# Keys and queries of batches 3 to 7 turned by the DMA crossbar instead of TensorE, with two output banks

## The chip, the cores and the metric

One core of one Trainium2 chip. The metric is the device time of one execution in microseconds (us), the median of several runs; most runs of one kernel lie within 0.3% of each other. "PE" is TensorE, "ACT" ScalarE, "DVE" VectorE, "POOL" GpSimd, "SP" the sync engine, whose queue ("SPq") issues most transfers. "L502" is line 502 of the kernel that the profile belongs to; the line numbers of two kernels differ.

## The reference

Local attention with a few global positions, then a feed-forward layer with softplus. Batch 8, 8 heads, sequence 576, head size 64, window 32, 8 global positions:

```python
scores = scale * np.matmul(q, k.transpose(0, 1, 3, 2))
mask = np.abs(pos[:, None] - pos[None, :]) <= window
mask = mask | is_global[:, None] | is_global[None, :]
scores = np.where(mask, scores, -1000000000.0)
attn = np.exp(scores - max); attn = attn / (sum(attn) + 1e-09)     # shortened
x = np.matmul(attn, v).transpose(0, 2, 1, 3).reshape(4608, 512)
h = x @ w_in                                                        # 512 -> 2048
out = softplus(h) @ w_out                                           # 2048 -> 512
```

## The kernel before

TensorE does two things in turns. The feed-forward layer runs over nine tiles of 512 tokens, each with 32 groups of four 128x512 matmuls, half of them hidden products ("hp") and half output products ("o") of the tile before. Between the groups, half step by half step, lies the attention of later batches, one pair of heads at a time: transposes of keys and queries, scores, sums of the exponentials ("av<-ex,ones") and values. A plan says in which half step each part is issued:

```python
STARTS = [33, 39, 45, 51, 57, 63, 70, 76] + [83 + 8 * i for i in range(4 * (B - 4) + 1)]
...
h, pair = STARTS[4 * b - 8 + p], STARTS[4 * b - 7 + p] - STARTS[4 * b - 8 + p]
to_transposes, to_scores, to_sums = h, h + pair // 2 + (pair == 7), h + pair
to_inverse, to_x = to_sums + 1, to_sums + 2
...
step(to_transposes, transposes, "k", b, p)
step(to_transposes + (b > 1), transposes, "q", b, p)
for grp in range(2):
    step(to_scores, scores, b, p, grp)
...
step(to_sums, inv_ln, b, p)       # ACT: logarithm of the row sums
step(to_inverse, inv_exp, p)      # ACT: exp(-log), the inverse
step(to_x, scale_x, b, p)         # DVE: values times inverse, into xT
```

So a pair takes 6 half steps in batch 2, 6 or 7 in batch 3, and 8 from batch 4 on. A half step is one group of four products. Keys and queries of a pair are turned by six matmuls each, into one PSUM bank, from where VectorE copies them into `KT` and `QT`:

```python
for r in range(RUN):
    for o, of in parts:
        nc.tensor.transpose(out=tb[o, r * NQ:(r + 1) * NQ], in_=of(r), identity=ident_bf[:NQ, :NQ])
...
copy(dst[:, p, 0:4, 0:KW].rearrange("p t (q r) -> p t q r", r=RUN), ...)   # VectorE, PSUM to SBUF
cg(dst[:, p, :, KW:P], g.unsqueeze(1).to_broadcast([P, NTL, NG]))         # GpSimd, global columns
```

An output tile collects in one PSUM bank through four half steps, and is then copied by VectorE and stored:

```python
ops[n] = psum["pool"].tile([P, d_model], FP32, tag="h" if last else "o", bufs=2 if last else 1, name="o")
products_out(n, i, op[:], range(4 * part, 4 * part + 4))
if part == 3:
    store(n, i, op[:])
```

The softmax here doesn't subtract the row's maximum and nothing guards it: scores larger than these inputs give would overflow.

Of the kernel before, what the change touches and what calls it, by code (L numbers as in the profile page):

```python
# [19 lines left out]
P = 128  # L20
WIN = 32
KW = 120
# [18 lines left out]
def kernel(  # L41
# [37 lines left out]
    KT = const.tile([P, NP, NTL, P], BF16)  # L79
    QT = const.tile([P, NP, NTL, P], BF16)  # L80
    V1 = [const.tile([P, NTL, HD], BF16, name=f"V1_{i}") for i in range(2)]
    runs = const.tile([NQ, H, RUN * D], FP32, name="k_f")
    v_f = const.tile([P, NTL, HD], FP32)
    GB = B - 3
    glob_2 = {n: const.tile([P, NP, NG], BF16, name=f"{n}_g2") for n in "kq"}
# [23 lines left out]
    def load_v(b, heads=slice(0, H)):  # L109
        for t in range(NTL):  # L110
            nc.sync.dma_start(out=v_f[:ST[t], t].rearrange("p (h d) -> p h d", d=D)[:, heads],
                              in_=v[b, heads, KW * t:KW * t + ST[t], :].rearrange("h s d -> s h d"))

    def load_v_rows(b):
        nc.sync.dma_start(out=v_f[KW:P], in_=v_rows[:, (b - 1) * HD:b * HD].unsqueeze(1).to_broadcast([NG, NTL, HD]))
# [171 lines left out]
    def transposes(n, b, p, copy=nc.vector.tensor_copy, unread=0):  # L287

        parts = [(slice(0, P), lambda r: kqb[n, b][:, r, p * P:(p + 1) * P])]
        if n == "q" and b < 2:  # L290
            parts = [(slice(64 * e, 64 * e + 64), lambda r, e=e: raw[b][:, 2 * p + e, r * D:(r + 1) * D]) for e in range(2)]
        if b == 1 and p:
            if n == "k":
                both[p] = region("tp")
            ps = both[p][:, 0:512] if n == "k" else both.pop(p)[:, 512:1024]
        else:
            ps = bank()[:]
        tb = ps.bitcast(BF16)
        for _ in range(unread):
            nc.tensor.matmul(out=ps, lhsT=junk[:, 0:P], rhs=junk[:], start=True, stop=True)  # L300
# [3 lines that stand above are left out]
        if b < 2:  # L304
            g = ps[:, 384:384 + NG]
            for r in range(RUN):
                for o, of in parts:
                    nc.tensor.matmul(out=g[o], lhsT=of(r), rhs=onehot[:NQ, r, :],
                                     start=(r == 0), stop=(r == RUN - 1), skip_group_check=True)
        else:  # L310
            copy = nc.vector.tensor_copy
            g = glob_2[n][:, p] if b == 2 else glob_T[n][:, p].rearrange("p (g b) -> p b g", b=GB)[:, b - B + GB]
        spread = lambda: spread_columns(n, b, p, tb, g, copy)
        if b == 1 and p:
            both.setdefault((p, "copies"), []).append(spread)
            if n == "q":
                for f in both.pop((p, "copies")):
                    f()
        else:
            spread()  # L320
# [22 lines left out]
    def products(b, p, grp):  # L343
        sc = SC[p, grp] = region("sc")[:].rearrange("p (e c) -> p e c", e=2)
        biased = (b, p) in BIASED
        if biased:
            for e in range(2):
                nc.tensor.matmul(out=sc[:, e, 0:GW[grp]], lhsT=ident_bf[:], rhs=biases[grp], start=True, stop=False,  # L348
                                 skip_group_check=True)
        for i, t in enumerate(GRP[grp]):  # L350
            w = WHI[t] - WLO[t]
            for e in range(2):
                r = slice(64 * e, 64 * e + 64)
                nc.tensor.matmul(out=sc[:, e, GOFF[t]:GOFF[t] + w], lhsT=KT[r, p, t, :],  # L354
                                 rhs=QT[r, p].rearrange("p t c -> p (t c)")[:, WLO[t]:WHI[t]],
                                 start=not biased, stop=(not biased or i == len(GRP[grp]) - 1), skip_group_check=biased)

    def exponentials(b, p, grp):
# [151 lines left out]
    def mm2(n, s):  # L510
        i, part = s // 4, s % 4
        if part == 0:

            last = n == n_tiles - 1
            ops[n] = psum["pool"].tile([P, d_model], FP32, tag="h" if last else "o", bufs=2 if last else 1, name="o")
        op = ops[n]
        if n == n_tiles - 1 and i == NT // P - 1:
            if part % 2 == 0:
                cols = slice(0, 256) if part == 0 else slice(256, 512)
                if part:  # L520
                    op = psum["pool"].tile([P, d_model], FP32, tag="h", bufs=2, name="o")
                products_out(n, i, op[:, cols], range(KF), cols)
                store(n, i, op[:, cols], cols)
            return
# [3 lines that stand above are left out]
# [31 lines left out]
    for i, n in enumerate("kq"):  # L559
        at(14 + i, 0, columns_of_2, n)  # L560
        at(27, i, global_columns, n)
        for g in range(NG):
            at(18 + g, 0, gather_rows, n, g)
    LOADS, CASTS = {3: (18, 20, 19)}, {3: (23, 26)}
    for b in range(1, B):
        g0 = 16 * (b - 1)
        if b > 2:
            loads = LOADS.get(b, (g0 - 22, g0 - 20, g0 - 17))
            at(loads[0], 1, load_runs, "k", b, every)
            at(loads[1], 1, load_runs, "q", b, every)  # L570
            at(loads[2], 1, load_v, b)
            at(loads[2], 1, load_v_rows, b)
            casts = CASTS.get(b, (g0 - 12, g0 - 9))
            for p in range(NP):
                for i, n in enumerate("kq"):
                    at(casts[0] + (4 * i + p) // 3, 0, cast_runs, n, b, pair_heads(p), nc.gpsimd.tensor_copy)
            for t in range(NTL):
                at(casts[1] + t // 3, 0, cast_v, b, t, nc.gpsimd)
        steps = {}

        def step(h, f, *a):
# [2 lines left out]
        for p in range(NP):  # L584
            if b == 1:

                to_transposes, to_scores, to_sums = (2 if p == 1 else 4 * p + 2), 4 * p + 4, 4 * p + 6
                to_inverse = to_x = to_sums
            else:
                h, pair = STARTS[4 * b - 8 + p], STARTS[4 * b - 7 + p] - STARTS[4 * b - 8 + p]  # L590
                to_transposes, to_scores, to_sums = h, h + pair // 2 + (pair == 7), h + pair
                to_inverse, to_x = to_sums + 1, to_sums + 2
            if (b, p) != (1, 0):
                step(to_transposes, transposes, "k", b, p)
                step(to_transposes + (b > 1), transposes, "q", b, p)
                for grp in range(2):
                    step(to_scores, scores, b, p, grp)
                for grp in range(2):
                    if (b, p) not in BIASED:
                        step(to_scores, mask, p, grp)  # L600
            step(to_sums, sums, b, p)
            step(to_sums, values, b, p)
            step(to_sums, inv_ln, b, p)
            step(to_inverse, glob_sums, b, p, 0)
            step(to_inverse, inv_exp, p)
            step(to_x, scale_x, b, p)
# [143 lines left out]
```

## Time and profile before

| | us | share of the span |
|---|---|---|
| time, median of 3 | 361.45 | |
| span of the profiled run | 358.5 | |
| TensorE busy | 340.8 | 95% |
| ScalarE busy | 271.6 | 76% |
| VectorE busy | 169.2 | 47% |
| GpSimd busy | 130.9 | 37% |

The busy line, the chain, the cost of the transposes and the pair periods stand in the prediction below. Two more views are needed. First the page's line for the transfers and its row of DMA shares (forty slices of the span, in tenths): after the first quarter the DMA engines are about half free.

```profile
DMA  7999999999546155806590658100000010010012
DMA packets 63252, 37.87 MB, mean 106 GB/s; under 512 B 41688, under 2 KB 58496, under 8 KB 63216
```

Then TensorE's waits between 60 and 130 us (what it waited for: us in all, times, longest):

```profile
PE sc L354 <- DVE xT L436: 1.6, 4, 0.5
PE o L502 <- DVE ot L507: 0.9, 1, 0.9
PE tp L303 <- DVE KT L327: 0.6, 2, 0.3
```

### The profile page before, as it was taken

How to read it: one execution, taken by the hardware profiler on the slowest of the kernel's cores; microseconds unless marked ns; L12 is line 12 of the kernel's file. 1: busy time of each engine (PE TensorE's matmuls, PEld its weight loads, DVE VectorE, ACT ScalarE, POOL GpSimd, SP SyncE). 2: the span in 40 equal slices, each digit the busy share in tenths (PEclk: the TensorE clock that was granted, in tenths of full speed). 3: DMA queues.
4: the chain of work that ended last, by engine and by line, in shares of the span. 5: the costliest groups of instructions: out<-in, count | busy, mean ns of one | idle time of the engine just before them, and what ended most of it. 6: DMA issues, size and time to landing. Idle time of an engine off the chain costs nothing.

```text
span 358.5 us, 7702 instructions
## 1 busy us (share of the span) xinstructions
PE 340.8 (95%) x2957; PEld 174.5 (49%) x2997; DVE 169.2 (47%) x477; ACT 271.6 (76%) x425; POOL 130.9 (37%) x301
## 2 busy tenths in 40 slices
PE   7898998999899999999999999999999999999996
PEld 3465554544355545554555455545554444444444
DVE  7864532565566565655566556555553200010021
ACT  3676998788789888888888888888888677776610
POOL 7953947896177016431744075304000100000000
PEclk9999999999999999999999999999999999999999
DMA  7999999999546155806590658100000010010012
GB/s 173 234 219 221 214 195 232 85 204 196 96 89 115 35 145 93 166 31 155 97 172 29 163 96 161 42 29 33 29 31 31 30 59 29 31 56 32 31 59 88
DMA packets 63252, 37.87 MB, mean 106 GB/s; under 512 B 41688, under 2 KB 58496, under 8 KB 63216
## 3 DMA queue, kind: packets, MB, share of 16 engines
q1 hardware_dynamic: 44912, 27.63, 32.4%
q0 software_dynamic: 18160, 9.75, 20.9%
q8 instruction: 23, 0.38, 0.5%
q14 instruction: 13, 0.11, 0.1%
q10 hardware_dynamic: 144, 0.01, 0.0%
HBM read 37.56 MB, written 9.55 MB: 131 GB/s over the span
## 4 chain that ended last, share of the span: by engine, by line
PE 77%; DVE 6%; ACT 5%; issue 4%; POOL 3%; DMA 3%; POOLq 0%; DVEq 0%; ACTq 0%
PE o L502 33%; PE hp L483 30%; PE av L396 6%; PE tp L303 4%; PE sc L354 4%; DMA k_f<-in_k_dram 3%; ACT ex L365 1%; DVE KT L325 1%; ACT rz L418 1%; DVE ot L507 1%; DVE xT L434 1%; POOL q_raw L107 1%; PE sc L348 1%; ACT rz L422 1%; POOL v_global_rows L126 1%
## 5 line engine op out<-in xcount | busy, mean ns | idle before, releaser
L483 PE MATMUL hp<-xT,w_in_t 128*128 128x512 bf16 x545 | 144.3, 380 | 3.9 <-ACT first_rz L489 1.0
L502 PE MATMUL o<-w_out_t,gt 128*128 128x512 bf16 (+1 forms) x585 | 144.5, 373 | 2.1 <-DVE ot L507 1.4
L495 ACT ACTIVATE e<-hp 128x512 f32<-128x512 f32 x128 | 76.5, 598 | 44.1 <-PE hp L483 40.9
L502 PEld LDWEIGHTS <-gt 128*128 128x128 bf16 x592 | 55.9, 98 | 63.3 <-issue 4.5
L496 ACT ACTIVATE gt<-e 128x512 bf16<-128x512 f32 x128 | 80.6, 630 | 4.1
L483 PEld LDWEIGHTS <-w_in_t 128*128 128x128 bf16 x576 | 52.1, 98 | 63.7 <-issue 5.8
L507 DVE COPY ot<-o 128x512 f32<-128x512 f32 (+1 forms) x37 | 25.0, 675 | 69.1 <-PE o L502 64.5
L455 POOL COPY xT<-xg 128x4 bf16 x64 | 16.4, 256 | 98.2 <-DVE xg L450 94.8
L365 ACT ACTIVATE ex<-sc 128x1008 bf16<-128x1008 f32 (+1 forms) x56 | 48.6, 919 | 0.7 <-PE sc L354 0.7
L374 DVE TENSOR_TENSOR ex<-ex,mask 128x1008 bf16<-128x1008 bf16 (+1 forms) x48 | 34.1, 714 | 25.2 <-ACT ex L365 24.3
L325 DVE COPY KT<-tp 128x480 bf16<-128x480 bf16 x31 | 20.3, 654 | 30.4 <-PE tp L303 21.7
L145 POOL CAST V<-v_f 128x512 bf16<-128x512 f32 (+3 forms) x45 | 22.0, 532 | 26.2 <-DMA v_f<-v_global_rows 21.3
L140 POOL CAST kb<-k_f 96x768 bf16<-96x768 f32 x30 | 25.6, 871 | 4.0 <-DMA k_f<-in_k_dram 4.0
L406 DVE TENSOR_REDUCE gs<-av 128x8 f32<-128x32 f32 x64 | 11.9, 186 | 30.7 <-ACT rz L418 27.2
L418 ACT ACTIVATE rz<-av 128x616 f32<-128x616 f32 x28 | 19.0, 680 | 7.1 <-PE av L396 6.5
L325 DVE COPY QT<-tp 128x480 bf16<-128x480 bf16 x29 | 19.0, 656 | 10.5 <-PE tp L303 9.8
L434 DVE TENSOR_TENSOR xT<-av,rz 128x480 bf16<-128x480 f32 x28 | 18.4, 656 | 11.6 <-ACT rz L422 11.4
L140 POOL COPY qb<-q_raw 96x768 bf16<-96x768 bf16 x24 | 19.3, 827 | 11.0 <-DMA q_raw<-in_q_dram 6.8
L354 PE MATMUL sc<-QT,KT 64*128 64x200 bf16 (+2 forms) x320 | 20.2, 241 | 2.7 <-DVE xT L436 1.6
L422 ACT ACTIVATE rz<-rz 128x616 f32<-128x616 f32 x28 | 19.7, 703 | 0.2
L354 PEld LDWEIGHTS <-KT 64*128 64x128 bf16 x320 | 10.6, 94 | 18.8 <-issue 14.7
L396 PE MATMUL av<-ex,ones 128*64 128x160 bf16 (+1 forms) x336 | 16.6, 233 | 0.3
(128 smaller groups left out, 282.0 us busy)
## 6 DMA issues: line engine op xcount, KB each, us to landing
out_dram<-ot SPq DMA_DIRECT2D x35, 256.0 KB, 2.0
v_f<-in_v_dram SPq DMA_DIRECT2D x24, 240.0 KB, 5.1
k_f<-in_k_dram SPq DMA_DIRECT2D x5, 1152.0 KB, 10.6
k_f<-in_k_dram SPq DMA_DIRECT2D x12, 288.0 KB, 7.4
q_raw<-in_q_dram POOLq DMA_DIRECT2D x6, 576.0 KB, 6.2
w_in_t<-in_moe_w_in_dram POOLq DMA_DIRECT2D x4, 512.0 KB, 7.2
w_out_t<-in_moe_w_out_dram POOLq DMA_DIRECT2D x4, 512.0 KB, 13.8
v_f<-in_v_dram SPq DMA_DIRECT2D x6, 192.0 KB, 5.4
```

What stands on the lines that cost most here:

```text
L140: copy(kqb[n, b][:, :, D * heads.start:D * heads.stop].rearrange("p r (h d) -> p h r d", d=D), (runs if n == "k" else raw[b])[:, heads].re ...
L325: copy(dst[:, p, 0:4, 0:KW].rearrange("p t (q r) -> p t q r", r=RUN), spread[:, 0:4 * NQT].rearrange("p (t q) r -> p t q r", q=NQT))
L354: nc.tensor.matmul(out=sc[:, e, GOFF[t]:GOFF[t] + w], lhsT=KT[r, p, t, :], rhs=QT[r, p].rearrange("p t c -> p (t c)")[:, WLO[t]:WHI[t]], s ...
L365: nc.scalar.activation(out=ex, in_=sc[:, :, 0:GW[grp]], func=ACTF.Exp, scale=SCALE)
L374: nc.vector.tensor_tensor(out=ex, in0=ex, in1=masks[grp][:, 0:GW[grp]].unsqueeze(1).to_broadcast([P, 2, GW[grp]]), op=ALU.mult)
L396: nc.tensor.matmul(out=av[64 * e:64 * e + 64, OFF + lo:OFF + hi], lhsT=weight(t, e), rhs=exps[p, grp][rows, e, c:c + hi - lo], start=(firs ...
L422: nc.scalar.activation(out=RZ[p], in_=RZ[p], func=ACTF.Exp, scale=-1.0)
L483: nc.tensor.matmul(out=hp[:], lhsT=w_in_t[:, kd, kf * P:(kf + 1) * P], rhs=xT[:, kd, n * NT:(n + 1) * NT], start=(kd == 0), stop=(kd == KD ...
L495: nc.scalar.activation(out=e[:], in_=hp[:], func=ACTF.Exp)
L496: nc.scalar.activation(out=gts[n][:, kf, :], in_=e[:], func=ACTF.Ln, bias=1.0)
L502: nc.tensor.matmul(out=op, lhsT=gts[n][:, kf, i * P:(i + 1) * P], rhs=w_out_t[:, kf, cols], start=(kf == 0), stop=(kf == KF - 1))
L507: nc.vector.tensor_copy(ot[:, cols], op)
```

## The change

The intent: take the transposes of batches 3 to 7 off the busiest engine. Keys and queries are loaded as token tiles (like the values, in rows of 256 bytes), cast to bf16 on GpSimd, and turned by a transposing DMA from SP's queue, straight into SBUF. Odd batches get buffers of their own, so that a batch can be turned while the one before is still read. The PSUM bank of the transposes is then free and takes every second output tile. The diff, cut to its core:

```diff
-    runs = const.tile([NQ, H, RUN * D], FP32, name="k_f")
+    kq_f = const.tile([P, H * RUN * D], FP32, name="kq_f")
+    runs = kq_f[:NQ].rearrange("p (h c) -> p h c", h=H)
...
+    def tokens(n, b):
+        if (n, b) not in tok:
+            fresh = b < 5
+            tok[n, b] = work.tile([P, NP * NTL * P], BF16, tag=f"{n}b", bufs=2, name=f"{n}t") if fresh else tok[n, b - 2]
+            if fresh:
+                nc.gpsimd.memset(tok[n, b][96:P], 0.0)
...
+    def turn(n, b):
+        if b % 2:
+            turned[n, b] = work.tile([P, NP, NTL, P], BF16, tag="raw", bufs=2, name=f"{n}T")
+        else:
+            turned[n, b] = KT if n == "k" else QT
+        nc.sync.dma_start_transpose(out=turned[n, b][:].rearrange("p a t c -> p (a t) c"), in_=tok[n, b][:])
...
-            ops[n] = psum["pool"].tile([P, d_model], FP32, tag="h" if last else "o", bufs=2 if last else 1, name="o")
+            ops[n] = psum["pool"].tile([P, d_model], FP32, tag="h" if last else "tp" if n and i % 2 else "o",
+                                       bufs=2 if last else 1, name="o")
...
+    def loads(b):          # k, q, v: five loads each, each cast two steps later; then k and q are turned
+        s0 = STARTS[4 * b - 8] // 2
+        if b == 3:
+            k0, kt, q0, qt, v0 = s0 - 12, s0 - 7, s0 - 8, s0 - 3, s0 - 5
...
-                step(to_transposes, transposes, "k", b, p)
-                step(to_transposes + (b > 1), transposes, "q", b, p)
+                if b < 3:
+                    step(to_transposes, transposes, "k", b, p)
+                    step(to_transposes + (b > 1), transposes, "q", b, p)
```

More of the change, by code (lines that the diff above doesn't have):

```diff
@@ L112, in load_v, with load_tokens, cast_tokens, spread_globals @@
                               in_=v[b, heads, KW * t:KW * t + ST[t], :].rearrange("h s d -> s h d"))
+    tok, turned = {}, {}
+    def tokens(n, b):
[4 more added lines that the diff above has]
+                nc.gpsimd.memset(tok[n, b][96:P], 0.0)
+        return tok[n, b][:].rearrange("p (a t c) -> p a t c", a=NP, t=NTL)
+    def load_tokens(n, b, t):
+        o = kq_f if n != "v" else v_f[:].rearrange("p t c -> p (t c)")
+        nc.sync.dma_start(out=o[:ST[t], t * HD:(t + 1) * HD].rearrange("p (h d) -> p h d", d=D),
+                          in_=src[n][b, :, KW * t:KW * t + ST[t], :].rearrange("h s d -> s h d"))
+    def cast_tokens(n, b, t):
+        nc.gpsimd.tensor_copy(tokens(n, b)[:ST[t], :, t, :],
+                              kq_f[:ST[t], t * HD:(t + 1) * HD].rearrange("p (a c) -> p a c", a=NP))
+    def turn(n, b):
[4 more added lines that the diff above has]
+        nc.sync.dma_start_transpose(out=turned[n, b][:].rearrange("p a t c -> p (a t) c"), in_=tok[n, b][:])
+    def spread_globals(n, b):
+        dst = turned[n, b]
+        g = glob_T[n][:].rearrange("p a (g b) -> p a b g", b=GB)[:, :, b - B + GB].unsqueeze(2)
+        if n == "k":
+            nc.gpsimd.tensor_copy(dst[:, :, :, KW:P], g.to_broadcast([P, NP, NTL, NG]))
+        else:
+            nc.gpsimd.tensor_copy(dst[:, :, 0:4, KW:P], g.to_broadcast([P, NP, 4, NG]))
+            nc.gpsimd.tensor_copy(dst[:, :, 4:5, ST[4]:ST[4] + NG], g)
     def load_v_rows(b):
@@ L311, in transposes @@
             copy = nc.vector.tensor_copy
-            g = glob_2[n][:, p] if b == 2 else glob_T[n][:, p].rearrange("p (g b) -> p b g", b=GB)[:, b - B + GB]
+            g = glob_2[n][:, p]
         spread = lambda: spread_columns(n, b, p, tb, g, copy)
@@ L349, in products @@
                                  skip_group_check=True)
+        kT, qT = turned.get(("k", b), KT), turned.get(("q", b), QT)
         for i, t in enumerate(GRP[grp]):
@@ L353, in products @@
                 r = slice(64 * e, 64 * e + 64)
-                nc.tensor.matmul(out=sc[:, e, GOFF[t]:GOFF[t] + w], lhsT=KT[r, p, t, :],
-                                 rhs=QT[r, p].rearrange("p t c -> p (t c)")[:, WLO[t]:WHI[t]],
+                nc.tensor.matmul(out=sc[:, e, GOFF[t]:GOFF[t] + w], lhsT=kT[r, p, t, :],
+                                 rhs=qT[r, p].rearrange("p t c -> p (t c)")[:, WLO[t]:WHI[t]],
                                  start=not biased, stop=(not biased or i == len(GRP[grp]) - 1), skip_group_check=biased)
@@ L563 @@
             at(18 + g, 0, gather_rows, n, g)
-    LOADS, CASTS = {3: (18, 20, 19)}, {3: (23, 26)}
+    def loads(b):
+        s0 = STARTS[4 * b - 8] // 2
+        if b == 3:
+            k0, kt, q0, qt, v0 = s0 - 12, s0 - 7, s0 - 8, s0 - 3, s0 - 5
+        elif b == 4:
+            k0, kt, q0, qt, v0 = s0 - 15, s0 - 10, s0 - 11, s0 - 6, s0 - 8
+        else:
+            k0, kt, q0, qt, v0 = s0 - 23, s0 - 15, s0 - 16, s0 - 8, s0 - 9
+        for n, first, last in (("k", k0, kt), ("q", q0, qt), ("v", v0, None)):
+            for t in range(NTL):
+                slot = first + (t // 2 if b < 5 else t)
+                at(slot, t % 2 if b < 5 else 1, load_tokens, n, b, t)
+                if n == "v":
+                    at(slot + 2, 1, cast_v, b, t, nc.gpsimd)
+                else:
+                    at(slot + 2, 0, cast_tokens, n, b, t)
+            if n == "v":
+                at(first, 0, load_v_rows, b)
+            else:
+                at(last, 0, turn, n, b)
+                at(max(last + 2, 28), 0, spread_globals, n, b)
     for b in range(1, B):
@@ L567 @@
         if b > 2:
-            loads = LOADS.get(b, (g0 - 22, g0 - 20, g0 - 17))
-            at(loads[0], 1, load_runs, "k", b, every)
-            at(loads[1], 1, load_runs, "q", b, every)
-            at(loads[2], 1, load_v, b)
-            at(loads[2], 1, load_v_rows, b)
-            casts = CASTS.get(b, (g0 - 12, g0 - 9))
-            for p in range(NP):
-                for i, n in enumerate("kq"):
-                    at(casts[0] + (4 * i + p) // 3, 0, cast_runs, n, b, pair_heads(p), nc.gpsimd.tensor_copy)
-            for t in range(NTL):
-                at(casts[1] + t // 3, 0, cast_v, b, t, nc.gpsimd)
+            loads(b)
         steps = {}
```

## The prediction

> **What bounds the kernel now.** I read the page first: the busy times, then the chain of work that ended last, then the groups of one operation. The busy line says that TensorE (PE) is almost never idle, and that ScalarE (ACT) is second. The chain line says the same thing in another way: 77% of the span is TensorE work that nothing else delayed.
>
> ```profile
> PE 340.8 (95%) x2957; PEld 174.5 (49%) x2997; DVE 169.2 (47%) x477; ACT 271.6 (76%) x425; POOL 130.9 (37%) x301
> PE 77%; DVE 6%; ACT 5%; issue 4%; POOL 3%; DMA 3%; POOLq 0%; DVEq 0%; ACTq 0%
> ```
>
> A shorter TensorE stream should therefore shorten the kernel, until another engine or a transfer takes over. So next I wanted the price of the part that goes away. The groups kept apart by shape show the transposes of the keys (kb) and of the queries that were cast on GpSimd (qb): 192 and 144 matmuls of 96 columns, with a mean of 206 ns, and hardly any idle time before them.
>
> ```profile
> L303 PE MATMUL tp<-ident_bf,kb 96*128 96x96 bf16 x192 | 13.5, 206 | 0.5 <-ACT kb L152 0.4
> L303 PE MATMUL tp<-ident_bf,qb 96*128 96x96 bf16 x144 | 10.1, 206 | 1.7 <-DVE KT L327 1.6
> ```
>
> A mean of 206 ns is a latency, not a price, because matmuls overlap. The price is read from the timeline, as the distance from the start of a group to the start of the next. This is one pair of heads in the settled part (from 173 to 182 us), then the one place at the start of a batch where the stream waits:
>
> ```profile
> 173.00 0.42 PE L303 MATMUL tp<-ident_bf,kb 96*128 96x96 bf16 x6
> 173.35 0.58 PE L396 MATMUL av<-ex,ones 128*64 128x160 bf16 x12
> 175.13 0.42 PE L303 MATMUL tp<-ident_bf,qb 96*128 96x96 bf16 x6
> 175.39 1.03 PE L502 MATMUL o<-w_out_t,gt 128*128 128x512 bf16 x4
> 178.08 0.56 PE L354 MATMUL sc<-QT,KT 64*128 64x160 bf16 x10
> ...
> 164.74 1.03 PE L483 MATMUL hp<-xT,w_in_t 128*128 128x512 bf16 x3
> 166.09 0.43 PE L303 MATMUL tp<-ident_bf,qb 96*128 96x96 bf16 x6 [0.32 <-DVE KT L327]
> ```
>
> Six key transposes cost 0.35 us (173.00 to 173.35), six query transposes 0.26 us (175.13 to 175.39). Last, the busy time in stretches of one pair each, so that the second engine is seen beside the first. The columns are the stretch, its length, and busy us of PE, PEld, DVE, ACT and POOL, then clock, DMA share and GB/s:
>
> ```profile
> 154.86:163.90 9.04, 8.99 (x82) 4.58 (x84) 5.02 (x13) 7.74 (x13) 1.87 (x6) 1.00 0.31 81
> 163.90:173.42 9.52, 9.15 (x83) 4.61 (x78) 5.39 (x15) 7.73 (x13) 3.85 (x15) 1.00 0.46 108
> 173.42:182.46 9.04, 8.99 (x80) 4.69 (x82) 5.52 (x13) 7.74 (x13) 6.85 (x12) 1.00 0.77 138
> ```
>
> A pair takes 9.04 us, the first of a batch 9.52; TensorE fills it, ScalarE has 7.74. The clock is 1.00 throughout.
>
> **What the Trainium skill says.** Three places. (1) "TensorE: Matmul & The Clock Gate", Part 4 on PE-mode transpose: a transpose is a matmul whose output goes to PSUM, so a VectorE copy must follow, at about 275 to 390 ns for 128x128. The trace agrees on the copy (654 ns for 480 columns and 246 for 96) and has less for the transpose, 206 ns; the trace counts. (2) "DMA: Bandwidth & Descriptors", section "DMA Transpose (X-bar)": the transposing DMA is issued from the sync or scalar queue, takes 2-byte types and writes SBUF. The change fits that: cast to bf16 first, then turned from the SP queue. (3) The same page, "Latency and other measured facts": 261 GB/s for a transposing DMA with a non-contiguous middle dimension. The kernel before has no such transfer, so no run here shows it. One turned tile is 128 x 2560 x 2 bytes = 655 KB; at that rate it is an estimated 2.5 us.
>
> **The change part by part.**
>
> Removed from TensorE: in batches 3 to 7, 5 x 4 = 20 pairs, with 12 transposes each. For an ordinary pair of batches 4 to 7: the step from the output products into the attention sums costs 0.1 us when it is direct (the change of tile shape, which is also seen ahead of the scores: 177.12 plus 0.86 for four products is 177.98, the scores start at 178.08), so the keys give back 0.35 - 0.10 = 0.25 and the queries 0.26. That is 0.51 us, 9.04 to 8.53. For the first pair of a batch: 0.26 for the keys, 0.26 for the queries, and the gap ahead of the queries, 166.09 - (164.74 + 0.87) = 0.48, which is there because the query transposes share one PSUM bank with the keys and wait for VectorE's copy. That is 1.00 us, 9.52 to 8.52. Both come to the same period, which speaks for the sum. Batches 4 to 7: 4 x (3 x 0.51 + 1.00) = 10.1 us.
>
> Batch 3 runs in a tighter plan, of pairs of 6 and 7 half steps. In 6-step pairs the scores already wait for VectorE's scaled output (0.51 and 0.40 us in two such pairs at 82 and 90 us), because it comes late in a chain from ACT. There only the key part comes back, 0.25; what the queries give up turns into more of this wait. In the two 7-step pairs I take 0.51. Batch 3: 1.5 us.
>
> Does the same wait catch the ordinary pairs? Counted from the start of the sums, after the change: the first hidden products 0.91 to 1.94 (end of the last matmul), exponential and logarithm on ACT to 3.15, the inverse to 3.85, VectorE's scaling to 4.75. TensorE reaches the scores at 4.47; the first 6 of the 10 products write the other PSUM region and need nothing of it, some 0.3 us, so the last 4 come at 4.77. It is met with nothing to spare. ACT, laid out the same way, ends its last logarithm at 9.05 and is next needed at 9.15. So ACT is 91% full (7.74 / 8.53) and still not the bound.
>
> Two output banks: the pages of waits put 0.5 us before TensorE's output products after 100 us, on VectorE's copy; in the stretch without attention each token block waits about 0.09 us (products due at 286.25 start at 286.34), for some nine blocks there. I take 0.9 us.
>
> Added, off the path: 20 x 2 x (0.654 + 0.246) = 36 us less for VectorE, and the GpSimd casts change from 8 x about 0.85 = 6.8 us to 10 x 0.64 = 6.4 us per batch, with four clearing writes once. Added on the DMA side: keys and queries now come in 256-byte rows, like the values. One such load of 1.18 MB ran at 184 to 190 GB/s when it was alone (182 to 186 us), so 6.4 us. Per batch 3 x 6.4 for the loads, 4 x 1.1 for the stores (256 KB at 232 GB/s), 2 x 2.5 for the turns: 29 us in a period of 34.1 us (3 x 8.53 + 8.52). It fits, at 85%. The issue plan leaves some 8 steps of 2.1 us between turning queries and the first scores for batches from 5 on, 5 steps for batch 3.
>
> Sum: 10.1 + 1.5 + 0.9 = 12.5 us. I take off 0.9 us for the crowded part below: 361.45 - 11.6 = 349.9 us.
>
> **The rivals.** (a) The transfers become the bound. For it: 85% is close; between 60 and 80 us the DMA share is already 1.27 to 1.74, and that is where batch 3's token loads start. A turned tile three times as slow, 7.5 us, would make a batch need 39 us of 34, 5 us too much in each of three batches; the slack of about 17 us would eat most of it. Result 350 to 360, in the bad case no gain. Against it: transfers overlap (shares to 1.3), and the plan starts them very early. (b) GpSimd blocks in order: it waits for a turn to land before it spreads the global columns, and behind it stand the writes of the global rows into the hidden layer's input. For batch 2 these come about 4 us before the second hidden tile needs them, behind a clearing write and four casts that each wait for a load. A stall of 1 to 4 us there: 351 to 354. (c) The scores wait for the scaled output in every pair, and the query half converts into waiting: 16 x 0.26 = 4.2 us less gain, 354. Against: the two PSUM regions. (d) SP's queue is in order, so a store waits behind a turn that waits for a cast. Against: two output buffers and 9 us between stores; no effect.
>
> **Range and chances.** All fine and no stall gives 349; (b) or (c) alone give up to 354; (a) gives up to 360. The range is 346.5 to 357. Faster than by 2% means under 354.2: 0.76. Within 2%: 0.20. Slower: 0.04.
>
> **What would show it.** Right: the pair period at 8.5 us, no transposes after batch 2, TensorE's busy share still 95% or more, and time lost nowhere in waits of TensorE for tiles written by DMA. Wrong by (a): TensorE idle before the scores with the turned tile or GpSimd's spread as releaser, and turns that take over 7 us to land. By (b): one stall of the hidden products near 100 us on GpSimd. By (c): idle before the scores on VectorE in most pairs, and a period near 8.8.

## The result, and the profile after

The changed kernel took 351.13 us (median of 4 runs, 350.70 to 352.70), the kernel before 361.47 us in the same session. The ratio is 0.9723, with a 95% interval of 0.9693 to 0.9753: faster. All ratios here are the mean time of one kernel's fast runs over that of the other's of the same rounds, so they aren't quite the ratio of the medians. In a later session the same kernel took 350.54 us, ratio 0.9689. The prediction was 349.9 in 346.5 to 357.

The page's busy line, its chain and its transfer line after the change:

```profile
PE 330.6 (95%) x2718; PEld 162.7 (47%) x2757; DVE 134.7 (39%) x397; ACT 269.8 (77%) x425; POOL 126.8 (36%) x265
PE 75%; DMA 8%; POOL 5%; issue 4%; ACT 3%; DVE 3%; SPq 0%; POOLq 0%; DVEq 0%; ACTq 0%
DMA packets 128169, 47.34 MB, mean 136 GB/s; under 512 B 114288, under 2 KB 123416, under 8 KB 128136
```

TensorE is 10.2 us less busy at the same 95%, so the time fell with it. VectorE lost 34.5 us and nothing came of that directly: it was not the bound. The packets doubled. The chain now has 8% of DMA and 5% of GpSimd in it, where the kernel before had 3% each: the reader should look for those places. To find them, lay the two traces side by side at the starts of the attention sums (us; each row is a stretch between two such starts):

| stretch | before | after | difference | predicted |
|---|---|---|---|---|
| start to the first sums of batch 2 | 69.44 | 69.96 | +0.52 | 0 |
| the other three pairs of batch 2 | 25.11 | 26.56 | +1.45 | +0.9 |
| batch 3, four pairs | 32.10 | 30.93 | -1.17 | -1.5 |
| batches 4 to 7, sixteen pairs | 146.79 | 137.78 | -9.01 | -10.1 |
| last sums to the end | 85.06 | 83.87 | -1.19 | -0.9 |
| span | 358.5 | 349.1 | -9.4 | -11.6 |

(The profiled run of the kernel before was one of its fastest, 360.14 us; by the medians the gain is 10.3 and 11.1 us in the two sessions.) The first row is start-up: both kernels do the same there, and the difference arises at 26 to 27 us, in a short stop of TensorE. The scores that follow start at 30.36 us here, at 29.84 in the kernel before, and at 29.75 to 29.85 in three later runs of the changed plan (r3, r10, r11). The first sums of batch 2 scatter all the same, for another wait of the start (near 37 us, for values that GpSimd casts): they start at 69.94 in r3, at 70.81 in r11 and at 70.62 in r9, which is the kernel before with a later edit. So this row is chance and not the change.

The prediction didn't say in which row its 0.9 us of crowd falls. The table sets it against batch 2, but the stall that it named, of the hidden products near 100 us, comes at 105.97 us (below) and so lies in the row of batch 3.

The settled part. These are two ordinary pairs and the windows that answer to those of before (stretch, length, busy us of PE, PEld, DVE, ACT, POOL, then clock, DMA share, GB/s):

```profile
144.95:153.54 8.59, 8.54 (x66) 4.03 (x66) 3.30 (x9) 7.62 (x13) 2.35 (x5) 1.00 0.96 179
170.73:179.32 8.59, 8.54 (x67) 4.03 (x67) 3.29 (x9) 7.62 (x13) 2.98 (x6) 1.00 1.22 213
```

From one start of the sums to the next, every pair from batch 4 on takes 8.59 us, but for the very first of batch 4 (8.91, and 10.08 before). Before, the first pair of a batch took 9.78 us, the next two 9.03 and the last 8.78. TensorE still fills the period. The prediction had 8.53, and the missing 0.06 us can be found in one place of the timeline, where ACT, DVE and PE meet:

```profile
173.87 0.70 ACT L460 ACTIVATE rz<-rz 128x616 f32<-128x616 f32 x1
175.18 0.25 DVE L474 TENSOR_TENSOR xT<-av,rz 128x96 bf16<-128x96 f32 x1
175.19 0.64 PE L392 MATMUL sc<-qT,kT 64*128 64x160 bf16 x10
175.76 1.04 PE L521 MATMUL hp<-xT,w_in_t 128*128 128x512 bf16 x4
```

The ten score products took 0.56 us before the change and take 0.64 now. The last four of them write the PSUM region from which VectorE scales its output; that ends at 175.43, and they wait for it: in the trace's single instructions the seventh product starts 0.29 us after the first here, and 0.23 us after it in the kernel before. It is too short a gap for the view of waits, so it shows only as a longer group.

The crowded part. TensorE's waits between 60 and 110 us in the changed kernel; the second and third are new:

```profile
PE sc L392 <- DVE xT L474: 1.8, 3, 0.8
PE tp L509 <- DMA hot_v<-in_k_dram: 1.4, 1, 1.4
PE hp L521 <- POOL xT L493: 0.8, 1, 0.8
```

From 110 us to the end TensorE's waits in this view are 0.5 us together. What GpSimd did ahead of the hidden products' wait (its copies of the global rows, "xT<-xg", come in its order, after a clearing write and a cast that waited for a load):

```profile
97.80 2.23 POOL L123 MEMSET kt<- 32x2560 bf16 x1
102.78 0.81 POOL L132 CAST kt<-kq_f 120x512 bf16<-120x512 f32 x1 [0.96 <-DMA kq_f<-in_k_dram]
103.55 2.38 POOL L493 COPY xT<-xg 128x4 bf16 x8
```

The casts also slow VectorE's masks, for which the sums wait once (0.4 us). The Trainium skill, "SBUF — State Buffer", section "Who interferes with whom", says that a VectorE instruction with two SBUF inputs contends with GpSimd instructions that read SBUF, not with those that only write it. The trace agrees: two masks together took 1.30 us beside a clearing write (at 76.66 us) and 1.80 us beside casts (at 68.81 us). Not every overlap shows it: a mask at 102.44 us, partly beside a cast, took 0.68 us, as long as a mask with GpSimd idle.

Last, what a turn costs the queue that issues it (count: min/median/max ns of one, and for all turns the time to landing in us):

```profile
L140 SPq DMA_TRANSPOSE kT<-kt x3: 3050/3587/4061, 74.2 to 198.7; - x3
DMA to landing us min/median/max: 4.8/5.3/6.9
```

SP is held some 3.6 us by one turn, and the tile lands 5.3 us after the issue. The prediction had 2.5 us, for the transfer alone. The turn issued at 106.48 us had the DMA engines to itself until 110 us; they moved 215 GB/s then, which makes an estimated 3.0 us for its 655 KB:

```profile
108.00:110.00 2.00, 2.00 (x18) 0.80 (x16) 0.82 (x2) 1.97 (x5) 1.90 (x3) 1.00 1.16 215
```

No score of TensorE waits for a turn.

### The profile page after: what moved, and what is told of

It reads as the page before. It is cut to its first block, busy times and chain, and to the rows that moved or that the text cites. A ratio compares the mean times of both kernels' runs of the same rounds, so it can differ in the third digit from the quotient of the medians.

```text
span 349.1 us, 7146 instructions
## 1 busy us (share of the span) xinstructions
PE 330.6 (95%) x2718; PEld 162.7 (47%) x2757; DVE 134.7 (39%) x397; ACT 269.8 (77%) x425; POOL 126.8 (36%) x265
## 4 chain that ended last, share of the span: by engine, by line
PE 75%; DMA 8%; POOL 5%; issue 4%; ACT 3%; DVE 3%; SPq 0%; POOLq 0%; DVEq 0%; ACTq 0%
PE o L540 32%; PE hp L521 32%; PE av L434 6%; PE sc L392 4%; DMA v_f<-in_v_dram 3%; DMA kq_f<-in_k_dram 3%; DMA q_raw<-in_q_dram 2%; ACT ex L403 1%; POOL xT L493 1%; PE tp L340 1%; DVE ex L412 1%; PE sc L385 1%; POOL q_raw L108 1%; POOL kt L123 1%; ACT first_rz L527 1%
## 5 line engine op out<-in xcount | busy, mean ns | idle before, releaser
L540 PEld LDWEIGHTS <-gt 128*128 128x128 bf16 x592 | 57.0, 98 | 66.0 <-issue 2.0
L412 DVE TENSOR_TENSOR ex<-ex,mask 128x1008 bf16<-128x1008 bf16 (+1 forms) x48 | 32.3, 678 | 21.2 <-ACT ex L403 20.1
L182 POOL CAST V<-v_f 128x512 bf16<-128x512 f32 (+3 forms) x45 | 22.9, 531 | 28.8 <-DMA v_f<-in_v_dram 27.1
L132 POOL CAST kt<-kq_f 120x512 bf16<-120x512 f32 (+1 forms) x25 | 15.4, 631 | 20.6 <-DMA kq_f<-in_k_dram 20.3
L132 POOL CAST qt<-kq_f 120x512 bf16<-120x512 f32 (+1 forms) x25 | 15.2, 621 | 17.1 <-DMA kq_f<-in_q_dram 17.0
L434 PEld LDWEIGHTS <-ones 128*64 128x64 bf16 x384 | 12.5, 109 | 11.4 <-issue 11.1
L434 PE MATMUL av<-ex,V 128*64 128x160 bf16 (+1 forms) x336 | 15.9, 229 | 0.0
L392 PE MATMUL sc<-QT,KT 64*128 64x200 bf16 (+2 forms) x200 | 13.4, 242 | 2.0 <-DVE xT L474 1.0
L434 PEld LDWEIGHTS <-V 128*64 128x64 bf16 x384 | 13.6, 110 | 1.1 <-issue 0.8
```

The costliest lines, as they stand in the source:

```text
L132: nc.gpsimd.tensor_copy(tokens(n, b)[:ST[t], :, t, :], kq_f[:ST[t], t * HD:(t + 1) * HD].rearrange("p (a c) -> p a c", a=NP))
L182: eng.tensor_copy(V1[b % 2][:rows, t, cols], v_f[:rows, t, cols])
L392: nc.tensor.matmul(out=sc[:, e, GOFF[t]:GOFF[t] + w], lhsT=kT[r, p, t, :], rhs=qT[r, p].rearrange("p t c -> p (t c)")[:, WLO[t]:WHI[t]], s ...
L412: nc.vector.tensor_tensor(out=ex, in0=ex, in1=masks[grp][:, 0:GW[grp]].unsqueeze(1).to_broadcast([P, 2, GW[grp]]), op=ALU.mult)
L434: nc.tensor.matmul(out=av[64 * e:64 * e + 64, OFF + lo:OFF + hi], lhsT=weight(t, e), rhs=exps[p, grp][rows, e, c:c + hi - lo], start=(firs ...
L540: nc.tensor.matmul(out=op, lhsT=gts[n][:, kf, i * P:(i + 1) * P], rhs=w_out_t[:, kf, cols], start=(kf == 0), stop=(kf == KF - 1))
```

## The experiments

Twelve kernels ran, all with correct results. The theory: the change gives TensorE's time back one for one, except for three small terms: the scores' wait for the scaled output, the crowd around batch 2, and the output bank. The rivals: the transfers or SP's queue are near a bound; GpSimd is late because of its own work.

**r1_after_again: the changed kernel unedited,** as the base for its session.

> The changed kernel once more, as the control of the other runs on this chip. 350.5 to 351.5 us. If the extra 0.5 us between 26 and 32 us, where both kernels run the same instructions, was chance, the first hidden product starts near 31.6 us in this profile; if it belongs to the kernel, near 32.1 us.

350.54 us (349.90 to 354.39, 6 runs), ratio 0.9689 (0.9668 to 0.9711). The result holds in another session. The first hidden product starts at 31.57 us, so the 0.5 us of start-up was chance. (The profiled run is the slowest of the six.)

**r2_one_bank: the second output bank taken back.**

```diff
-            ops[n] = psum["pool"].tile([P, d_model], FP32, tag="h" if last else "tp" if n and i % 2 else "o",
+            ops[n] = psum["pool"].tile([P, d_model], FP32, tag="h" if last else "o",
```

> The change without its second output bank. My sum gave the second bank 0.9 us, so 352.0 us, with the output products again waiting some 0.09 us per token block in the stretch without attention. Rival: the bank is worth nothing there (VectorE is now idle enough), 351.1 us. Second rival: it is worth more than 2 us because the attention part needs it too, 353 us or more.

352.45 us (352.18 to 354.71), ratio 0.9767. Against r1 that is 1.9 us by the medians. The trace places 1.27 of it in the stretch after the last sums: 85.14 us against 83.87. There is no attention there; one boundary between two output tiles looks like this with one bank (the output products at 285.24 follow a finished tile, 0.94 us after the hidden products began, where 0.86 is the normal step):

```profile
284.30 1.03 PE L521 MATMUL hp<-xT,w_in_t 128*128 128x512 bf16 x4
285.24 1.02 PE L540 MATMUL o<-w_out_t,gt 128*128 128x512 bf16 x4
```

So it goes at eight boundaries of the tail, by 0.08 us each, and at the first one, at 271.27 us, by 0.7. The pair period is 8.59 either way. So the bank is worth more than the 0.9 us predicted, 1.2 to 1.9; what makes up the part that is not in the tail was not settled, since the crowded part scatters by as much.

**r3_early_inverse: the inverse of the row sums half a step earlier on ACT,** so that VectorE scales sooner.

```diff
-                to_inverse, to_x = to_sums + 1, to_sums + 2
+                to_inverse, to_x = to_sums, to_sums + 2
```

> ScalarE takes the inverse's exponential straight after its logarithm, in the 0.67 us in which it waits for the hidden products, so VectorE's scaled output is ready over 1 us earlier. If the 0.06 us by which each pair is longer than my 8.53 us (8.59), and the waits of 0.5 to 0.8 us in the short pairs near 75, 83 and 101 us, come from the scores waiting for the scaled output, the period falls to 8.53 and the time by 16 x 0.06 + 1.8 = 2.8 us, to 348.3 us. Rival: the 0.06 us is the pipeline's own (a change of tile shape between score groups), the period stays at 8.59 and only the short pairs gain, 349.3 us. Second rival: ScalarE is the bound by now, and the move shifts the wait into the first hidden products: 351 us.

348.83 us (five runs 348.34 to 349.08, one 352.96), ratio 0.9666. Five of the six runs of r1, on the same chip in the same rounds, lie between 349.90 and 351.38, so the two do not overlap there; with the outlier of each kept, the intervals of the ratios do. The trace is clear. ACT does the inverse right after the logarithm, VectorE ends at 172.07, and the scores come 1.5 us later and take 0.56 us again:

```profile
170.49 0.72 ACT L460 ACTIVATE rz<-rz 128x616 f32<-128x616 f32 x1
171.82 0.25 DVE L474 TENSOR_TENSOR xT<-av,rz 128x96 bf16<-128x96 f32 x1
173.62 0.56 PE L392 MATMUL sc<-qT,kT 64*128 64x160 bf16 x10
```

The period is 8.52, in fifteen of the sixteen pairs (8.83 in the first). This shows that the 0.06 us per pair is the scores' wait, the prediction's rival (c) at a quarter of the 0.26 us that it feared. The gain over r1 is 1.7 us by the medians, where 2.8 was expected: the sixteen pairs give 1.2, and the waits of the scores in the short pairs fall from 1.8 to 0.3 us, but the hidden products' wait for GpSimd grows from 0.8 to 1.1. It is also the fastest kernel.

**r4_turn_twice: every turn issued twice.**

```diff
         nc.sync.dma_start_transpose(out=turned[n, b][:].rearrange("p a t c -> p (a t) c"), in_=tok[n, b][:])
+        nc.sync.dma_start_transpose(out=turned[n, b][:].rearrange("p a t c -> p (a t) c"), in_=tok[n, b][:])
```

> Each turn is issued twice, the second over the first, so ten more transposing transfers of 655 KB, some 3.5 us each on SP's queue and 5.3 us to landing. If the transfers have room (my sum: 29 us of work in 34 us), the time stays within 1 us of 351.1, or loses 1 to 2 us in the crowded part before 110 us. If the DMA is the bound behind the wall (rival a), five pairs of turns add up to 5 us per batch and the time goes to 358 us or more, with idle time before the scores.

382.00 us, ratio 1.0572: 31 us slower than r1, a miss for both expectations. But the DMA share did not rise with it (0.91 between 200 and 260 us, at 179 GB/s; the unedited kernel has 0.91 between 130 and 240 us, at 162). The waits of SP's queue show what came late:

```profile
SPq L140 <- POOL qt L132: 21.5, 4, 6.7
SPq L140 <- POOL V L183: 19.6, 4, 5.9
SPq L141 <- DMA kT<-kt: 5.8, 3, 2.4
```

SP issues in order. The second turn (L141) writes the same tile and so waits for the first to land, and everything behind it in the queue, the next loads and then the casts and turns that need them, comes later: turns wait for casts on GpSimd (L140). TensorE in the end waits for values, gathered rows and spread columns, and where it idled the granted clock was lower too (0.83 to 0.91 in stretches of 20 us with under 17 us of matmuls, 0.99 to 1.00 in those with over 18). A stretch of that run (columns as above; clock 0.83):

```profile
180.00:200.00 20.00, 14.25 (x90) 6.33 (x87) 5.19 (x17) 10.27 (x17) 7.93 (x20) 0.83 1.03 196
```

Each second turn adds to the queue a wait of 1.8 us on average and 3.1 us of its own issue. It also lets the tile land some 5 us later, and GpSimd, which works in order and waits for the landing, stands 51 us in all for turned tiles, where it was 13. This run doesn't separate the cost of the transfer from the cost of these waits; r7 tries to.

**r5_uncrowd: global rows gathered earlier, clearing writes on VectorE.**

```diff
-                nc.gpsimd.memset(tok[n, b][96:P], 0.0)
+                nc.vector.memset(tok[n, b][96:P], 0.0)
...
-            at(18 + g, 0, gather_rows, n, g)
+            at(14 + g // 2, 0, gather_rows, n, g)
```

> The four clearing writes of the token tiles (2.23 us each on GpSimd) go to VectorE, and the sixteen gathers of the later batches' global rows are issued before batch 3's casts instead of between them. If the changed kernel loses its 1.2 us against my sum because GpSimd, in order, comes late in the crowded part (1.4 us before the transposes of the gathered rows, 0.8 us before the second hidden tile), both waits go and the time falls by 1.5 to 2.5 us, to 348.5 to 349.5 us. Rival: GpSimd only waits for transfers there (the DMA is the cause), so the wait returns under another name and the time stays within 0.5 us of 350.9.

363.74 us, ratio 1.0062: a miss. The edit made a wait of its own. The gathers are issued from GpSimd, whose work is in order; placed earlier they stood ahead of batch 2's global columns and waited for the values' transfers, and TensorE's scores at 78.56 waited 11.2 us for the columns. The run says nothing of the crowd, only that GpSimd's order is tight there.

**r6_queries_only: queries turned by DMA, keys on TensorE as before, one output bank.** The edit is long: keys keep the loads and casts of the kernel before, and

```diff
             if (b, p) != (1, 0):
+                step(to_transposes, transposes, "k", b, p)
                 if b < 3:
-                    step(to_transposes, transposes, "k", b, p)
                     step(to_transposes + (b > 1), transposes, "q", b, p)
```

> Half of the change: only the queries are turned by the crossbar, the keys stay on TensorE, so there is one output bank. By the steps of the prediction the queries are worth 3 x 0.26 + 0.74 us in each of batches 4 to 7, 6.1 us, and up to 0.5 us in batch 3, less the crowd: the time is near 355.5 us, and the pair period in the settled part 8.78 us or a little more. Rival: without the keys' part the queries' part is eaten by the wait for the scaled output, the period stays above 8.95 us and the time above 358 us.

375.30 us, ratio 1.0404. Another miss in the time: the two orders of loads, it seems, didn't fit together, and scores waited 13.7 us for GpSimd's copies into `KT`. Its undisturbed pairs still answer the question: a batch takes 9.10 + 8.85 + 8.85 + 8.60 = 35.40 us, between 36.62 before and 34.36 after. So the queries are worth 1.2 us in a batch and the keys 1.0. The prediction had 4 x 0.26 + 0.48 = 1.52 and 0.25 x 3 + 0.26 = 1.01: the keys fit, and the queries lack 0.3, about the wait of the scores in four pairs (4 x 0.06); the score groups last 0.64 us in this run too. An ordinary pair takes 8.85 us, nearer to the expected 8.78 than to the rival's 8.95.

**r7_extra_copy: behind every turn a copy of 655 KB from DRAM to DRAM, on the same queue,** which nothing waits for.

```diff
+        nc.sync.dma_start(out=scratch.rearrange("(t p) d -> p t d", p=P),
+                          in_=src[n][b].rearrange("h s d -> (h s) d")[0:2560].rearrange("(t p) d -> p t d", p=P))
```

> Behind each turn, SP also issues a copy from memory to memory of 655 KB in 256-byte rows that nobody waits for: the bytes of a second turn without its blocking of SP's queue. Turning twice cost 31 us. If the DMA engines have no room left, this costs much the same, 15 us or more. If what was lost there was SP's in-order queue, blocked for two turns one after the other, while loads stood behind them, this costs under 4 us and the mean DMA share rises by about a tenth.

358.38 us, ratio 0.9939: 7.8 us slower than r1 (which ran on another chip), between the two expectations. Of the 6.8 us by which the two spans differ, 5.2 are lost by the last sums of batch 3 (132.61 against 127.45), in the crowded part, where one pair takes 13.61 us. In the settled part the transfers rise from 162 to 209 GB/s (130 to 240 us), and their share from 0.91 to 1.02; three of the sixteen pairs take 8.83 to 9.68 us and the others keep 8.59. So the settled part could take 29% more traffic at a cost of some 1.8 us, and the crowded part had no room. The copy moves as many bytes as a second turn of 655 KB, but nothing waits for it; r4 lost four times as much. So r4's loss is mostly not the traffic but the order: SP's queue held longer, and GpSimd waiting for the later landing. Which of these two weighs more was not tested. (A copy in DRAM is not the same transfer as a turn in SBUF, so the split is not exact.)

**r8_one_turned: one buffer of turned tiles,** each turn after the last scores of the batch before.

```diff
-        if b % 2:
-            turned[n, b] = work.tile([P, NP, NTL, P], BF16, tag="raw", bufs=2, name=f"{n}T")
-        else:
-            turned[n, b] = KT if n == "k" else QT
+        turned[n, b] = KT if n == "k" else QT
...
+                free = (STARTS[4 * b - 9] + 4) // 2 + 1
+                at(max(last, free), 0, turn, n, b)
+                at(max(last + 2, 28, free), 1, spread_globals, n, b)
```

> One buffer of turned tiles: every batch is turned into the same two tiles, so a turn can only be issued after the batch before has had its last scores, about 4 steps (8.6 us) before its own first. Keys and queries need 3.5 us each of SP's queue and 5.3 us to landing, plus GpSimd's spread, some 10 us: I expect TensorE to stall 1 to 4 us before the first scores of batches 4 to 7, 355 to 367 us. Rival: the two buffers are not needed, under 353 us.

366.30 us, ratio 1.0120, as expected. Here the turn's 5 us do lie on the path, once a batch:

```profile
PE sc L389 <- POOL QT L145: 12.3, 5, 5.5
POOL KT L143 <- DMA KT<-kt: 23.8, 5, 8.9
```

Without the second buffer, in this plan, the change is 1.2% slower than the kernel before (ratio 1.0075 to 1.0165). The buffer is what hides a turn of 5.3 us.

**r9_before_early_inverse: the edit of r3 in the kernel before.**

> The kernel before, with the inverse of the row sums one half step earlier (the same edit as in r3, without the change). Theory: the wait of the scores for the scaled tile is met with no slack in ordinary pairs of the kernel before, because its transposes of keys and queries fill that time, so the edit gives only the few waits of the tight pairs of batches 2 and 3 (about 0.5 us each, three or four pairs): 359.5 to 360.5, a ratio of 0.994 to 0.998. Rival: the edit helps any plan alike, also without the change, by the 1.7 us seen in r3: below 359.8 together with periods of ordinary pairs under 9.0. A period of ordinary pairs that stays at 9.03 is for the theory.

361.77 us (median of the five fast runs; the sixth, 367.42 us, was slow) against 361.42 before, ratio 1.0001 (0.9986 to 1.0017): nothing, less than the theory had expected. Ordinary pairs stay at 9.03, as the theory said. The first pair of a batch even grew, from 9.78 to 10.08 us, and the reason is in the line that waited 0.32 us in the prediction's timeline: the query transposes need VectorE to have emptied the bank that they share with the keys. The plan issues two short reductions of VectorE together with the inverse, so the edit moved them too, and they now stand ahead of that copy: it starts 1.04 us after the key transposes (167.18 - 166.14), where it was 0.74 (165.22 - 164.48).

```profile
168.05 0.43 PE L303 MATMUL tp<-ident_bf,qb 96*128 96x96 bf16 x6 [0.61 <-DVE KT L327]
```

So in this plan the early inverse pays only once the transposes are gone.

**r10_best and r11_clears_first: the clearing writes made once, by VectorE, before the main loop** (r10 with the early inverse, r11 without).

```diff
+    pair_of_tiles = {(n, i): work.tile([P, RUN * HD], BF16, tag=f"{n}b{i}", bufs=1, name=f"{n}t{i}")
+                     for n in "kq" for i in range(2)}
...
-                nc.gpsimd.memset(tok[n, b][96:P], 0.0)
...
+    for t in pair_of_tiles.values():
+        nc.vector.memset(t[96:P, 0:NP * NTL * P], 0.0)
```

> The changed kernel with the early inverse of r3, and with its four clearing writes made once by VectorE before the main loop instead of by GpSimd between 65 and 100 us. Theory: the clearing writes are what makes GpSimd late in the crowded part, so the waits there for the spread columns (1.4 us), for the hidden tile with the global rows (0.8) and for the mask (0.4) shrink: 346.3, at most 347.5. Rival: GpSimd is late there because its casts wait for loads, and the clearing writes lie in time it would have waited anyway: 348.3 to 349, with the same waits in the profile.

> The changed kernel with only the clearing writes moved, the inverse where the change has it. Theory: as in the run above, 2 us less than the changed kernel's 350.5, thus 348 to 349, the settled period unchanged at 8.59. Rival: no difference, 350 to 351.

349.71 us (ratio 0.9683) and 350.21 us (0.9694). Against 348.83 and 350.54 with the clearing writes in place, on another chip, that is no gain. The rival was right, and GpSimd's timeline in r10 shows why: the casts, no longer behind a clearing write, wait for their loads instead, and the copies of the global rows start at 103.84, where they started at 103.55. The crowd's two waits are still there in r10, 1.6 us before the transposes of the gathered rows and 1.1 before the hidden products; in r11 they are 2.2 and 0.2.

```profile
102.84 1.05 POOL L129 CAST kt<-kq_f 120x512 bf16<-120x512 f32 x1 [1.88 <-DMA kq_f<-in_k_dram]
103.84 2.11 POOL L492 COPY xT<-xg 128x4 bf16 x7
```

**r12_from_batch_4: token tiles only from batch 4 on,** with the early inverse of r3. Batch 3 keeps the loads and transposes of the kernel before.

```diff
-        if b > 2:
-            loads(b)
+        if b == 3:
+            ...                    # loads and casts of the kernel before
+        elif b > 3:
+            loads(b)
...
-                if b < 3:
+                if b < 4:
                     step(to_transposes, transposes, "k", b, p)
```

> The changed kernel with the early inverse of r3, but with token tiles only from batch 4: batch 3 keeps the loads, casts and TensorE transposes of the kernel before (and the second output bank starts one tile later, since the transposes hold it; batch 5's key loads start later, for their buffers). Theory: the waits of the crowded part for the gathered rows (1.3 to 1.4 us) and for the hidden tile with the global rows (1.4 to 1.7 us) come from batch 3's token loads, which share the DMA engines with batch 2's values, so both vanish, batch 2's pairs take 25.1 to 25.3 us from the first sums to batch 3's first (25.48 in r3), and batch 3's pairs 32.0 to 32.3 instead of 30.83; the settled period is 8.52. Sum: 349 to 350.5, so batch 3 gains about one us by the change after all its costs. Rival: batch 4's token loads now meet batch 3's values and the same waits only move some 20 us later: batch 3 over 33 us and 351 or more.

350.64 us (350.21 to 351.02), ratio 0.9705. Both waits are gone between 60 and 135 us; these are all of TensorE's over 0.5 us there:

```profile
PE o L540 <- DVE ot L545: 1.5, 1, 1.5
PE tp L340 <- DVE KT L364: 0.6, 1, 0.6
```

The three pairs of batch 2 take 24.72 us, less than before the change (25.11) and than in r3 (25.48). Batch 3 takes 32.66, more than expected, for its transposes and the copies that they wait for (30.83 in r3). Together 57.38 against 56.31 us in r3, both counted from the first sums of batch 2 to the last of batch 3. So the crowd was made by batch 3's token tiles, and it did not move on to batch 4. The theory puts it down to their loads; the run takes their loads, casts and turns away together, so it doesn't show which. By these two traces, turning batch 3 by DMA costs 0.8 us in batch 2, gives 1.8 in batch 3, and is worth about 1.1 us. (The kernel before took 32.10 us in batch 3; against that the gain there is 1.3.)

## Why the prediction was right

**The bound.** TensorE bounded the kernel before and does so after; taking matmuls off it shortened the kernel by 10.3 to 11.1 us, with 11.6 predicted. All four steps that made it right hold: the price of the transposes read from the distance of groups in the timeline, the wait ahead of the first pair's queries that goes too, a period that becomes the same for all pairs of a batch, and the loads that fit in the free half of the DMA time, outside the crowded part. The total is nearer by the medians (0.5 to 1.3 us short) than by the two traces (2.2 us short), because the profiled run of the kernel before was a fast one.

**Ordinary and first pairs.** 8.59 us for both kinds, with 8.53 and 8.52 predicted. The mechanism is right and one term was wrong: "the first 6 of the 10 products ... some 0.3 us, so the last 4 come at 4.77". The six take 0.23 us, so by this sum the last four come at 4.70, ahead of the scaled output that was foreseen for 4.75. Measured from the same start, the scaling ends at 4.70 and the four start at 4.75, 0.06 us late. Sixteen of these are 1.0 us, nearly the whole difference in batches 4 to 7 (-9.01 for -10.1). r3 took the wait away and got the predicted 8.52. One reading doesn't hold: the prediction's 9.52 and 9.04 us for the first pair and the pair before it come from a window edge at 163.90 us, 0.33 us after the sums that start there. From sums to sums it is 9.78 and 8.78. The four pairs of a batch add up to the same 36.6 us, so the sum isn't touched.

**Batch 3.** -1.17 us for -1.5, with a stall of 0.8 us in it that the prediction had priced apart (the crowd, below); without it the four pairs gain 1.9. The reason is right in part: the scores' wait for the scaled output does grow, but in one pair, from 0.2 to 0.8 us (at 101.27 us). The 0.51 and 0.40 us from which this was argued (at 82 and 90 us) belong to batch 2. With r12 as the base, where batch 3 has its transposes and the rest is turned, the four pairs gain 1.8 us (32.66 to 30.83), and against the kernel before 1.3 (32.10); in r12 the second bank starts one tile later too, so not all of it need be the transposes.

**Output banks.** Predicted 0.9; measured 1.2 to 1.3 in the tail by the traces, 1.9 by the medians with r2. The prediction's own two readings, 0.5 and nine times 0.09, add up to 1.3.

**The crowd.** "I take off 0.9 us for the crowded part": the stall that it foresaw (rival b: GpSimd's copies of the global rows come late, and hidden products wait near 100 us) came, with 0.8 us at 105.97. But batch 2 lost another 1.45 us that was not foreseen: the longest new wait there was for the gathered rows, a transfer (1.4 us at 92 us). By the prediction's own sign, "time lost nowhere in waits of TensorE for tiles written by DMA", this part was wrong. Of the causes named in (b), the clearing write was not one: r10 and r11 show that GpSimd would have waited for loads in that time. r12 shows that both waits come with batch 3's token tiles.

**The turn.** "At that rate it is an estimated 2.5 us": too short. Its transfer takes an estimated 3.0 us at the 215 GB/s measured, it holds SP for some 3.6, and it lands 5.3 us after the issue. For the sum of transfers on the DMA engines that is a small error (about 30 us for 29, in a period of 34.4); of the time from the issue until the tile can be used, 2.5 us is less than half. The mean DMA share, 0.91 between 130 and 240 us, can't be held against the sum's 85%, for a load that ran alone already shows 1.30 (182 to 186 us of the kernel before). The prediction's sign for rival (a), over 7 us to land, was nearly reached (6.9), and still no score waited, because of the second buffer and the early start: r8 shows what it is without the first. A reader should see that the prediction was saved here by slack and not by the estimate.

**SP's order.** Rival (d) was put at "no effect", which is right for the change. r4 shows how near it is: a second turn behind each, some 5 us more of that queue and a tile that lands some 5 us later, cost 31 us.

## What to carry to other kernels

When the busiest engine sheds work, the gain is the distance between group starts in the timeline, not the mean duration. What limited the next step here was a chain that had been met with no slack: lay such a chain out to a tenth of a microsecond, and move its first link earlier in the same change. A slow transfer cost nothing here as long as a second buffer and an early issue hid it, so check buffers and queue order ahead of rates. And where loads are pulled forward, price the stretch into which they are pulled: that is where this change gave back 0.8 to 1.5 us in batch 2 alone.

## What the Trainium skill lacked or had wrong

- "DMA: Bandwidth & Descriptors", section "Issuing engines are not separate DMA queues", says that the sequencer's time to start a transfer "is usually small relative to the DMA itself". For the transposing DMA here it isn't: 3.0 to 4.7 us of SP's queue, of 5.3 us (median) to landing for 655 KB.
- The same page, "Latency and other measured facts": 261 GB/s for a transposing DMA, on one kernel. The turn here that had the engines to itself ran at 215 GB/s. From issue to landing a turn took 4.8 to 6.9 us, among other transfers; no page has that time for a turn of 655 KB.
- "TensorE: Matmul & The Clock Gate", Part 4: about 275 ns for one 128x128 transpose in a kernel's context, and no price for a stream of them. Here six in a row (96 rows, 96 columns) cost 0.26 us of TensorE together, though one lasts 206 ns.
